# Scores of the first batch from turned q and k in float32, in one product instead of three float16 ones, and a larger weight of the longest chain in the order of work

## The chip, the cores and the metric

The kernel runs on one core of one Trainium2 chip. The metric is the device time of one execution in microseconds (us), the median of several runs. Lower is better.

## The reference

The program is attention with rotary position embedding, followed by a two-layer perceptron. There are 4 batches of 8 heads, 576 positions and 64 values per head:

```python
q_rot, k_rot = rotate(q), rotate(k)                # x1*cos - x2*sin, x1*sin + x2*cos
scores = q_rot @ k_rot.T / sqrt(64)
attn = exp(scores - max(scores)); attn /= sum(attn) + 1e-9
x = (attn @ v)                                     # all heads side by side: 2304 x 512
h = x @ w_in                                       # 2304 x 2048
out = (h * tanh(softplus(h))) @ w_out              # 2304 x 512
```

q and k have a standard deviation of about 0.58, and all inputs are float32.

## The kernel before, in words

**Layout.** Two heads make a pair P (16 pairs, four to a batch). The turned q and k of a pair lie with 128 partitions, 64 rows for each of its heads, and 576 columns. A step (P, t) makes 128 rows of scores for both heads (t = 0 to 3; 2 x 576 columns); the fifth, t = 4, holds the last 64 rows of both heads in one tile of 576 columns. Steps 0 and 1 make block 0 of a pair (256 tokens), steps 2 to 4 block 1 (320 tokens). All pairs of a batch do block 0 first, then block 1. The perceptron takes a batch in the same two blocks, so there are eight chunks of it; each needs the attention output of all four pairs of its block.

**Turning (`rope_turn`, line 387).** SP loads raw q or k (with the halves swapped beside it) into the tile raw0 or raw1, of which there is one each (L389). For batch 0 only, DVE takes its largest absolute value (L393). The products with cos and sin (L399) and their sum (L402), in two halves of 288 columns, run on POOL or DVE, whichever the planner finds sooner. The sum is written over the raw tile.

**Parts (`prep`, line 410).** A float32 number is written as two float16 parts, after a multiplication by a power of two. ScalarE (ACT) makes the first part (L418), DVE the second (L420), both from the raw tile into the tile qk. DVE then copies the last 64 columns of k of each head onto the diagonal of a tile kd (L427), so that one product with 128 rows makes the last 64 columns of the scores of both heads, the tails.

**The power of two (`max_exponents` line 359, `pow2` line 376, `qk_scale` line 684).** DVE reduces the largest values (L362), PE turns them into a row (L365), DVE reduces the row (L367), takes the exponent and bounds it (two L340), spreads it on a diagonal (L371), PE broadcasts it (L373), and DVE makes four factors (L340) and the factor `unit` that takes them back (L690). In batch 0 this runs once for each pair, in `prep_first` (line 675); later batches have one scale for a batch.

**Scores (`scores`, line 450).** Three float16 products (first by first, second by first, first by second part) go into PSUM for each head: 512 columns with 64 rows per head (L461), then the tails (L470). There are two PSUM tiles `psc`, which scores, the transposes of the weights and the first layer of the perceptron share. Then (`exponentials`, line 491) DVE takes the maximum (L495), ACT scales it (L497) and makes the exponentials (L501), both with `unit` as their scale, read from memory.

**Weights and values.** In batch 0 the weights stay float32: PE transposes them (L534, L536), ACT or DVE copies them out (L546, L547), and float32 products with v make the output (L610, L612, L613; L612 and L613 write the two column halves). Later batches use two float16 parts and DMA transposes (L583).

**Perceptron weights.** w_in and w_out come as 64-bit words in quarters and eighths (L779, L810) into tiles that are used for other things later. DVE takes their largest value (L697), PE and DVE find the power of two, and a decode of ACT, POOL and DVE instructions (L710, L718 or L719, L722, L725, then L731, L732, L735) makes two float16 parts. A buffer is free for the next load after L725 has read it. The layers themselves are L876 and L912, three float16 products each.

**The order.** All operations are recorded first, each with an estimated duration, the engines that may do it, and what it reads and writes. A planner (`Plan.order`, line 123) then simulates the engines and issues, on each, the ready operation of the lowest priority number. That number is the operation's place in the recorded order minus ALPHA times the length in us of the longest chain behind it. The issue order on each engine is fixed by it. ALPHA is 26. All loads go through SP's queue, in order.

Of the kernel before, what the change touches and what calls it, by code (L numbers as in the profile page):

```python
# [10 lines left out]
F32 = mybir.dt.float32  # L11
# [7 lines left out]
AF = mybir.ActivationFunctionType  # L19
# [15 lines left out]
RING = 4  # L35
# [9 lines left out]
QS = 0  # L45
NX = 4
TR = 107 / 128
ALPHA = 26
COUNT = [10, 10, 10, 10, 10, 10, 10, 0]
BURST = 2  # L50
SLOT0 = [15, 17, 18, 20, 22, 23, 25, 26, 28]
# [207 lines left out]
def dve_ns(n):  # L259
    return 1.04 * n + 65  # L260
# [23 lines left out]
def attention_mish_mlp(ctx: ExitStack, tc: tile.TileContext, qk, v, flat, rope, ident_in, w_in, w_out, outT):  # L284
# [11 lines left out]
    def fixed(shape, dt, name, planned=True):  # L296
        return Buf(lambda: const.tile(list(shape), dt, name=name), planned=planned)
# [12 lines left out]
    w2 = fixed((128, 4, 2, NF, 128), F16, "w2")  # L310
    w2e = [Buf(lambda e=e: w2()[:, e]) for e in range(4)]
    kdiag = [fixed((128, 2, 128), F16, f"kd{r}") for r in range(RING)]
    for t in (*kdiag, cs, ident, ones, cells, w1, w2):
        t()
    def psc():

# [5 lines left out]
    def small(shape=(128, 1), dt=F32):  # L322
        at = sc.get("n", 0)
        sc["n"] = at + shape[1]
        return Buf(lambda: cells()[0:shape[0], at:at + shape[1]].bitcast(dt))
# [61 lines left out]
    def rope_turn(P, j):  # L387
        t = sbuf((128, 2, S), F32, f"raw{j}", 1)
        load("qk", dma_ns(128 * 2 * S * 4), lambda dma: dma(t(), qk[P][:, 2 * j:2 * j + 2]),  # L389
             w=[(t, 0), (t, 1), (t, 2), (t, 3)])  # L390
        if P < NP:
            am = sc["qkam", P]
            op((DVE, dve_ns(S), lambda: nc.vector.tensor_reduce(  # L393
                am()[:, j:j + 1], t()[:, 0], axis=AX.X, op=ALU.max, apply_absolute_value=True)), w=[(am, j)], r=[(t, 0), (t, 1)])
        for c in range(2):
            s = slice(c * HS, (c + 1) * HS)

            def mul(e, s=s):
                e.tensor_tensor(out=t()[:, :, s], in0=t()[:, :, s], in1=cs()[:, :, s], op=ALU.mult)  # L399

            def add(e, s=s):
                e.tensor_tensor(out=t()[:, 0, s], in0=t()[:, 0, s], in1=t()[:, 1, s], op=ALU.add)  # L402

            op([(POOL, pool_ns(S), lambda f=mul: f(nc.gpsimd)), (DVE, dve_ns(S), lambda f=mul: f(nc.vector))],
               w=[(t, c), (t, 2 + c)], r=[cs], port=True)
            op([(POOL, pool_ns(HS), lambda f=add: f(nc.gpsimd)), (DVE, dve_ns(HS), lambda f=add: f(nc.vector))],
               w=[(t, c)], r=[(t, 2 + c)], port=True)
        return t

    def prep(P, j):  # L410


        t = st.pop(("T", P, j)) if P < NP else rope_turn(P, j)
        if j == 0:
            st["QK", P] = sbuf((128, 4, S), F16, "qk", RING)
        o = st["QK", P]
        s = sc["qk", P if P < NP else -(P // NP)][j]
        op((ACT, act_ns(S, ptr=1), lambda: nc.scalar.activation(o()[:, 2 * j], t()[:, 0], AF.Copy, scale=f32(s))),  # L418
           w=[(o, 2 * j)], r=[(t, 0), (t, 1), s])
        op((DVE, dve_ns(S) + 61, lambda: nc.vector.scalar_tensor_tensor(  # L420
            out=o()[:, 2 * j + 1], in0=t()[:, 0], scalar=f32(s), in1=o()[:, 2 * j], op0=ALU.mult, op1=ALU.subtract)),
           w=[(o, 2 * j + 1)], r=[(t, 0), (t, 1), s, (o, 2 * j)], port=True)
        if j == 1:
            d = st["KD", P] = Buf(kdiag[P % RING], [st["KD", P - RING]] if P >= RING else ())
            for h in range(2):
                own = slice(64 * h, 64 * h + 64)
                op((DVE, 200, lambda own=own: nc.vector.tensor_copy(d()[own, :, own], o()[own, 2:4, 512:S])),  # L427
                   w=[(d, h)], r=[(o, 2), (o, 3)], port=True)
# [21 lines left out]
    def scores(P, t):  # L450


        QK, kd = st["QK", P], st["KD", P]
        pt = psc()
        passes = ((0, 2), (1, 2), (0, 3))

        def fn():
            def mm(h, q, keys, to, rows=slice(0, 128)):
                own = slice(64 * h, 64 * h + 64)
                for a, (i, j) in enumerate(passes):  # L460
                    yield lambda a=a, i=i, j=j: nc.tensor.matmul(  # L461
                        pt()[rows, to:to + keys.stop - keys.start], QK()[own, i, q], QK()[own, j, keys], start=a == 0, stop=a == 2)

            if t < 4:
                q = slice(128 * t, 128 * t + 128)
                for one in zip(*[mm(h, q, slice(0, 512), 1024 * h) for h in range(2)]):
                    for f in one:
                        f()
                for a, (i, j) in enumerate(passes):
                    nc.tensor.matmul(tails(pt), QK()[:, i, q], kd()[:, j - 2], start=a == 0, stop=a == 2)  # L470
            else:
                q, A, B_ = slice(512, S), slice(0, 64), slice(64, 128)
                a = [*mm(0, q, slice(0, 512), 0, A), *mm(0, q, slice(512, S), 512, A)]
                b = [*mm(1, q, slice(0, 448), 64, B_), *mm(1, q, slice(512, S), 0, B_), *mm(1, q, slice(448, 512), 512, B_)]
                for f in (a[0], b[0], a[1], b[1], a[2], b[2], *b[3:6], a[3], b[6], a[4], b[7], a[5], b[8]):
                    f()

        op((PE, 6 * 150, fn), w=[pt], r=[(QK, k) for k in range(4)] + [(kd, h) for h in range(2)])
        return pt

    def both(pt, n):
# [4 lines left out]
    def tails(pt):  # L486

        x = pt()
        return bass.AP(tensor=x.tensor, offset=x.offset + 512, ap=[x.ap[0], [448, 2], [1, 64]])

    def exponentials(P, t, sm):
        n, unit = 2 if t < 4 else 1, sc["unit", P if P < NP else -(P // NP)]
        pt = scores(P, t)
        m = sbuf((128, 2), F32, "mx", 4)
        op((DVE, dve_ns(n * S), lambda: nc.vector.tensor_reduce(  # L495
            m()[:, :n], both(pt, n), axis=AX.X, op=ALU.max, negate=True)), w=[m], r=[pt])
        op((ACT, 220, lambda: nc.scalar.activation(m()[:, :n], m()[:, :n], AF.Copy, scale=unit())), w=[m], r=[unit])  # L497
        es = []
        for h in range(n):
            e = sbuf((128, S), F32, f"e{h}", 2)  # L500
            op((ACT, 850, lambda h=h, e=e: nc.scalar.activation(  # L501
                e(), pt()[:, 960 * h:960 * h + S], AF.Exp, bias=m()[:, h:h + 1],
                scale=unit(), accum_out=sm()[:, h:h + 1])), w=[e, (sm, h)], r=[pt, m, unit], table="exp")
            es.append(e)
        return es

# [167 lines left out]

    def prep_first(P):

        sc["qkam", P] = small((128, 2))
        for j in range(2):
            st["T", P, j] = rope_turn(P, j)
        qk_scale(P, 1)  # L680
        for j in range(2):
            prep(P, j)

    def qk_scale(b, n=3):

# [333 lines left out]

    nc.scalar.preload_act_table_set("exp_and_others")  # L1020
    nc.vector.memset(ones(), 1.0)
    for t in kdiag:
        nc.vector.memset(t(), 0.0)
    program()
    with tc.manual_schedule():
# [56 lines left out]
```

## Time and profile before

| | |
|---|---|
| median of 3 runs | 714.83 us (713.12 to 715.37) |
| the profiled execution | 716.38 us |
| its span, first to last instruction | 714.6 us |
| mean granted TensorE clock | 0.938 |
| busy: PE / DVE / ACT / POOL | 613.4 / 489.5 / 459.7 / 218.6 us |

PE is TensorE, DVE VectorE, ACT ScalarE, POOL GpSimd, SP the queue that issues the loads. A row of groups gives a line of the kernel, the engine, the operation, output and input tiles with their shapes, how often it ran, then the busy time in us and the mean of one in ns. A clock of 1.00 is 2.4 GHz, 0.50 is 1.2 GHz; values between are a mean over a stretch. Neighbouring instructions on an engine overlap a little in their recorded spans.

### The profile page before, as it was taken

To read this page: it belongs to the slowest core of one execution; us is meant where nothing else is said; L and a number is where in the kernel's file an instruction comes from. 1 tells how busy PE (TensorE), PEld (TensorE's weight loads), DVE (VectorE), ACT (ScalarE), POOL (GpSimd) and SP (SyncE) were. 2 spreads that over 40 slices of the span, in tenths; PEclk is the share of its full clock that TensorE was granted. 3 is DMA by queue.
4 is the path that set the end of the run, shared out by engine and by line. 5 is a ranking of instruction groups with operands and counts; after the bars stand their busy time and mean duration, and the time that the engine had idled before them with its cause. 6 is when DMAs were issued, how large, how long until landed. Compare 5 with 4: busy or idle time off the path is not lost.

```text
span 714.6 us, 13150 instructions
## 1 busy us (share of the span) xinstructions
PE 613.4 (86%) x5069; PEld 423.8 (59%) x5069; DVE 489.5 (69%) x904; ACT 459.7 (64%) x974; POOL 218.6 (31%) x209
## 2 busy tenths in 40 slices
PE   1446776975779999999979899999799999998997
PEld 0223444753456776677656566777566667776775
DVE  6999988798879586748956987478747584471210
ACT  2636778784667567758765776788657775682520
POOL 3344542115445411303551632024534020020000
PEclk9957886997789999999999999999999999999999
DMA  9824560350344584936598649456861294345000
GB/s 355 349 98 167 186 177 23 104 141 1 127 132 111 160 188 117 172 63 128 124 190 223 173 113 175 82 126 115 168 150 34 61 166 86 60 94 103 1 11 28
DMA packets 162416, 90.78 MB, mean 127 GB/s; under 512 B 129585, under 2 KB 150193, under 8 KB 162353
## 3 DMA queue, kind: packets, MB, share of 16 engines
q1 hardware_dynamic: 157744, 85.22, 49.3%
q10 hardware_dynamic: 4608, 4.72, 2.1%
q8 instruction: 40, 0.66, 0.4%
q14 instruction: 24, 0.19, 0.1%
HBM read 53.35 MB, written 4.72 MB: 81 GB/s over the span
## 4 chain that ended last, share of the span: by engine, by line
PE 53%; DVE 22%; DMA 11%; ACT 9%; issue 3%; SPq 1%; POOL 0%; POOLq 0%; ACTq 0%; DVEq 0%
PE psc L876 19%; PE pp L912 16%; PE psc L461 5%; PE po L622 4%; DVE mx L495 3%; DMA et<-ew 3%; ACT e L501 3%; DMA w<-in_w_out 3%; DMA stg<-in_v 2%; PE po L912 2%; DVE ew L522 2%; DVE mr L725 2%; DVE cells L697 2%; DVE qk L420 1%; PE psc L470 1%
## 5 line engine op out<-in xcount | busy, mean ns | idle before, releaser
L876 PE MATMUL psc<-xt,w 128*128 128x256 f16 (+1 forms) x1536 | 195.7, 287 | 6.8 <-ACT mh L880 4.3
L912 PE MATMUL pp<-g,w 128*128 128x256 f16 (+1 forms) x1440 | 190.4, 287 | 8.4 <-ACT ot L920 4.4
L876 PEld LDWEIGHTS <-w 128*128 128x128 f16 x1536 | 150.3, 98 | 47.6 <-issue 9.4
L912 PEld LDWEIGHTS <-w 128*128 128x128 f16 x1536 | 147.6, 98 | 50.6 <-issue 14.3
L501 ACT ACTIVATE e<-psc,mx,cells 128x576 f32<-128x576 f32 x144 | 118.3, 824 | 4.8 <-DVE ew L522 2.2
L516 POOL TENSOR_SCALAR ew<-e,rs 128x576 f16<-128x576 f32 x66 | 53.9, 823 | 220.0 <-DVE rs L512 201.5
L495 DVE TENSOR_REDUCE mx<-psc 128x2 f32<-128x1152 f32 (+1 forms) x80 | 98.0, 1231 | 24.5 <-PE psc L470 16.4
L522 DVE SCALAR_TENSOR_TENSOR ew<-e,rs,ew 128x576 f16<-128x576 f32 x108 | 92.5, 888 | 17.5 <-POOL ew L516 12.5
L880 ACT ACTIVATE mh<-psc,cells 128x256 f32<-128x256 f32 (+1 forms) x128 | 62.7, 498 | 62.2 <-PE psc L876 57.9
L897 DVE SCALAR_TENSOR_TENSOR g<-mh,cells,g 128x512 f16<-128x512 f32 (+1 forms) x64 | 58.1, 910 | 59.5 <-ACT g L894 59.2
L399 POOL TENSOR_TENSOR raw<-raw,cs 128x576 f32<-128x576 f32 x45 | 69.3, 1555 | 70.9 <-DMA raw<-in_qk 51.5
L461 PE MATMUL psc<-qk 64*128 64x512 f16 (+3 forms) x624 | 73.6, 356 | 14.0 <-ACT e L501 8.4
L497 ACT ACTIVATE mx<-mx,cells 128x2 f32<-128x2 f32 (+1 forms) x80 | 23.4, 292 | 49.1 <-DVE mx L495 48.2
L735 POOL TENSOR_TENSOR w<-mr,w 128x512 f16<-128x512 f32 x22 | 26.5, 1210 | 83.3 <-ACT w L731 67.2
L461 PEld LDWEIGHTS <-qk 64*128 64x128 f16 (+1 forms) x624 | 26.1, 102 | 42.7 <-issue 25.9
L623 PE MATMUL po<-et,v 128*64 128x320 f16 (+1 forms) x288 | 46.7, 301 | 0.5 <-DMA et<-ew 0.5
L402 POOL TENSOR_TENSOR raw<-raw 128x288 f32<-128x288 f32 x49 | 43.8, 912 | 11.0 <-DVE raw L399 8.2
L622 PE MATMUL po<-et,v 128*64 128x320 f16 (+1 forms) x288 | 47.0, 301 | 0.0
L894 ACT ACTIVATE g<-mh,cells 128x640 f16<-128x640 f32 (+1 forms) x59 | 45.8, 776 | 1.7
L518 ACT ACTIVATE ew<-e,rs 128x576 f16<-128x576 f32 x42 | 31.7, 767 | 11.7 <-DMA et<-ew 5.9
L666 DVE TENSOR_REDUCE cells<-stg 128x1 f32<-128x768 f32 x30 | 28.0, 944 | 15.6 <-DMA stg<-in_flat 15.6
L622 PEld LDWEIGHTS <-v 128*64 128x64 f16 x288 | 28.6, 113 | 14.1 <-issue 9.4
(102 smaller groups left out, 787.7 us busy)
## 6 DMA issues: line engine op xcount, KB each, us to landing
raw<-in_qk SPq DMA_DIRECT2D x32, 576.0 KB, 4.5
stg<-in_flat SPq DMA_DIRECT2D x30, 384.0 KB, 3.8
w<-in_w_in SPq DMA_DIRECT2D x6, 1024.0 KB, 12.7
w<-in_w_out SPq DMA_DIRECT2D x5, 1024.0 KB, 5.9
stg<-in_v SPq DMA_DIRECT2D x12, 320.0 KB, 3.7
stg<-in_w_out SPq DMA_DIRECT2D x6, 512.0 KB, 4.5
out_dram<-ot ACTq DMA_DIRECT2D x16, 160.0 KB, 2.8
g<-in_w_in SPq DMA_DIRECT2D x2, 1024.0 KB, 9.1
```

The costliest lines, as they stand in the source:

```text
L399: e.tensor_tensor(out=t()[:, :, s], in0=t()[:, :, s], in1=cs()[:, :, s], op=ALU.mult)
L461: yield lambda a=a, i=i, j=j: nc.tensor.matmul(pt()[rows, to:to + keys.stop - keys.start], QK()[own, i, q], QK()[own, j, keys], start=a == ...
L495: op((DVE, dve_ns(n * S), lambda: nc.vector.tensor_reduce(m()[:, :n], both(pt, n), axis=AX.X, op=ALU.max, negate=True)), w=[m], r=[pt])
L501: op((ACT, 850, lambda h=h, e=e: nc.scalar.activation(e(), pt()[:, 960 * h:960 * h + S], AF.Exp, bias=m()[:, h:h + 1], scale=unit(), accum ...
L516: op([(POOL, 1.27 * S, lambda: nc.gpsimd.tensor_scalar(w()[:, c], e(), r()[:, h:h + 1], 1.0, op0=ALU.mult, op1=ALU.mult)), (ACT, act_ns(S, ...
L522: op((DVE, dve_ns(S) + 61, lambda: nc.vector.scalar_tensor_tensor(out=w()[:, c], in0=e(), scalar=r()[:, h:h + 1], in1=w()[:, hc], op0=ALU. ...
L622: nc.tensor.matmul(po()[0:64, :n], V()[:, vi, c, 0:64], et[:, c, :n], start=False, stop=last)
L623: nc.tensor.matmul(po()[64:128, :n], V()[:, vi, c, 64:128], et[:, 5 + c, :n], start=False, stop=last)
L876: nc.tensor.matmul(hp(), w1()[:, wi, cc, f:f + 128], x()[:, xi, cc], start=cc == 0 and a == 0, stop=cc == NCC - 1 and a == 2)
L880: op((ACT, act_ns(n, psum=True, ptr=1), lambda j=j, hp=hp: nc.scalar.activation(hn()[:, j, :n], hp(), AF.Mish, scale=uh())), w=[(hn, j)], ...
L897: op((DVE, dve_ns(2 * n) + 61, lambda: nc.vector.scalar_tensor_tensor(out=out(1), in0=hn()[:, :, :n], scalar=f32(gs), in1=out(0), op0=ALU. ...
L912: nc.tensor.matmul(pp()[:, :n], w2e[e]()[:, wi, f], g()[:, gi, f % 8, :n], start=f == 0 and a == 0, stop=f == NF - 1 and a == 2)
```

## The change

Pairs 0 to 3 (P < NX = 4, the first batch) keep turned q and k in float32. The largest values, the powers of two and the float16 parts are gone for them; the sum of the rotation writes straight into the tile qk, which is now float32 of the same size. A float32 tile per pair holds the diagonal. One float32 product per head and one for the tails make the scores, and the constant 1/8 takes the place of `unit`. The planner's estimate for the scores of such a step goes from 900 to 1100 ns, and ALPHA from 26 to 35, for all operations of the kernel.

```diff
-ALPHA = 26
+ALPHA = 35
...
+    kwide = [fixed((128, 128), F32, f"kw{r}") for r in range(NX)]
...
 def rope_turn(P, j):
...
-        if P < NP:
-            am = sc["qkam", P]
-            op((DVE, dve_ns(S), lambda: nc.vector.tensor_reduce(
-                am()[:, j:j + 1], t()[:, 0], axis=AX.X, op=ALU.max, apply_absolute_value=True)), w=[(am, j)], r=[(t, 0), (t, 1)])
+        wide = st["QK", P] if P < NX else None
...
-                e.tensor_tensor(out=t()[:, 0, s], in0=t()[:, 0, s], in1=t()[:, 1, s], op=ALU.add)
+                e.tensor_tensor(out=wide()[:, j, s] if wide else t()[:, 0, s], in0=t()[:, 0, s], in1=t()[:, 1, s], op=ALU.add)
...
 def scores(P, t):
...
-        passes = ((0, 2), (1, 2), (0, 3))
+        exact = P < NX
+        passes = ((0, 1),) if exact else ((0, 2), (1, 2), (0, 3))
...
-                    nc.tensor.matmul(tails(pt), QK()[:, i, q], kd()[:, j - 2], start=a == 0, stop=a == 2)
+                    nc.tensor.matmul(tails(pt), QK()[:, i, q], kd() if exact else kd()[:, j - 2],
+                                     start=a == 0, stop=a == len(passes) - 1)
...
-                for f in (a[0], b[0], a[1], b[1], a[2], b[2], *b[3:6], a[3], b[6], a[4], b[7], a[5], b[8]):
+                for f in (a[0], *b[:2], a[1], b[2]) if exact else (a[0], b[0], a[1], b[1], a[2], b[2], *b[3:6], a[3], b[6], a[4], b[7], a[5], b[8]):
...
-        op((PE, 6 * 150, fn), w=[pt], r=[(QK, k) for k in range(4)] + [(kd, h) for h in range(2)])
+        op((PE, 1100 if exact else 6 * 150, fn), w=[pt], r=[(QK, k) for k in range(4)] + [(kd, h) for h in range(2)])
...
 def exponentials(P, t, sm):
-        n, unit = 2 if t < 4 else 1, sc["unit", P if P < NP else -(P // NP)]
+        n, unit = 2 if t < 4 else 1, None if P < NX else sc["unit", -(P // NP)]
+        units = [] if unit is None else [unit]
+
+        def scale():
+            return D ** -0.5 if unit is None else unit()
...
 def prep_first(P):
-        sc["qkam", P] = small((128, 2))
+        o = st["QK", P] = sbuf((128, 2, S), F32, "qk", RING)
         for j in range(2):
-            st["T", P, j] = rope_turn(P, j)
-        qk_scale(P, 1)
-        for j in range(2):
-            prep(P, j)
+            rope_turn(P, j)
+        d = st["KD", P] = kwide[P]
+        for h in range(2):
+            own = slice(64 * h, 64 * h + 64)
+            op((DVE, 150, lambda own=own: nc.vector.tensor_copy(d()[own, own], o()[own, 1, 512:S])),
+               w=[(d, h)], r=[(o, 3)], port=True)
...
-    for t in kdiag:
+    for t in (*kwide, *kdiag):
         nc.vector.memset(t(), 0.0)
```

## Rows read from the trace of the kernel before

**Rows 1.** Busy time of each engine by stage: the stage in us and its length; then for each engine the busy us and, in brackets, its instructions; then the mean granted clock of TensorE, the share of the DMA engines and GB/s.

```profile
0.00:9.00 9.00, 0.37 (x1) 0.08 (x1) 3.84 (x12) 1.28 (x1) 1.54 (x5) 1.00 0.81 305
9.00:98.00 89.00, 48.64 (x289) 28.11 (x291) 82.54 (x183) 51.72 (x113) 42.09 (x38) 0.78 0.60 219
98.00:222.00 124.00, 94.35 (x711) 62.53 (x708) 105.19 (x244) 88.02 (x205) 45.74 (x42) 0.82 0.33 95
222.00:660.00 438.00, 419.21 (x3700) 296.68 (x3698) 290.89 (x459) 300.60 (x629) 129.26 (x126) 0.99 0.61 128
660.00:714.60 54.60, 50.84 (x375) 36.40 (x372) 7.08 (x8) 18.05 (x29) 0.00 (x0) 1.00 0.04 15
```

The engines stand in the order PE, PE's weight loads, DVE, ACT, POOL.

**Rows 2.** The loads on SP's queue: two lines of the waits of the whole span (what waited, for what: us in total, times, longest us), then the issue of the third pair's raw q and k in order of time (start us, length us).

```profile
SPq L810 <- DVE mr L725: 83.5, 9, 28.1
SPq L389 <- DVE qk L420: 41.1, 8, 9.6
...
43.83 1.06 SPq L389 DMA_DIRECT2D raw<-in_qk  x2
```

**Rows 3.** DVE in order of time, with the first score product on PE: start us, length us, the instruction, and in brackets the idle time before it and what ended it. Neighbours of one kind are merged (x2, x4).

```profile
4.60 0.76 DVE L393 TENSOR_REDUCE cells<-raw 128x1 f32<-128x576 f32 x1 [3.05 <-DMA raw<-in_qk]
...
12.39 1.42 DVE L402 TENSOR_TENSOR raw<-raw 128x288 f32<-128x288 f32 x2
...
14.98 0.80 DVE L420 SCALAR_TENSOR_TENSOR qk<-raw,cells,qk 128x576 f16<-128x576 f32 x1
...
15.33 1.12 PE L461 MATMUL psc<-qk 64*128 64x512 f16 x4 [3.79 <-ACT qk L418]
...
16.96 0.80 DVE L420 SCALAR_TENSOR_TENSOR qk<-raw,cells,qk 128x576 f16<-128x576 f32 x1
...
18.55 0.57 DVE L427 COPY kd<-qk 64x128 f16<-64x128 f16 x2
...
20.35 1.35 DVE L495 TENSOR_REDUCE mx<-psc 128x2 f32<-128x1152 f32 x1
...
41.93 0.35 DVE L340 TENSOR_SCALAR cells<-po 128x1 int32<-128x1 f32 x4
...
42.98 1.55 DVE L420 SCALAR_TENSOR_TENSOR qk<-raw,cells,qk 128x576 f16<-128x576 f32 x2
```

**Rows 4.** Groups of DVE instructions in the first 80 us: busy us and mean ns, then the idle time before them. Of the 18 on `po`, 16 belong to the chains of the first batch.

```profile
L420 DVE SCALAR_TENSOR_TENSOR qk<-raw,cells,qk 128x576 f16<-128x576 f32 x8 | 6.3, 813 | 0.7 <-ACT qk L418 0.6
L393 DVE TENSOR_REDUCE cells<-raw 128x1 f32<-128x576 f32 x8 | 5.9, 745 | 3.7 <-DMA raw<-in_qk 3.7
L427 DVE COPY kd<-qk 64x128 f16<-64x128 f16 x8 | 2.0, 246 | 0.1
L371 DVE TENSOR_SCALAR cells<-ident,cells 2x2 f32<-2x2 f32 x4 | 1.8, 456 | 0.0
L340 DVE TENSOR_SCALAR cells<-po 128x1 int32<-128x1 f32 x18 | 1.7, 144 | 0.9 <-PE po L373 0.7 <-PE po L356 0.3
L367 DVE TENSOR_REDUCE cells<-po 2x1 f32<-2x128 f32 x4 | 1.1, 273 | 0.0
L690 DVE TENSOR_SCALAR cells<-cells 128x1 f32<-128x1 f32 x4 | 0.8, 207 | 0.0
L362 DVE TENSOR_REDUCE cells<-cells 128x2 f32<-128x2 f32 x4 | 0.6, 149 | 0.0
L340 DVE TENSOR_SCALAR cells<-cells 2x1 int32<-2x1 int32 x4 | 0.5, 134 | 0.0
```

**Rows 5.** PE in order of time: two steps' scores at full clock (88.33) and at half clock (83.38), float32 products on a column half (75.96 to 77.04, six of a run), and float32 transposes of 128 columns.

```profile
75.96 0.38 PE L612 MATMUL po<-et,v 128*64 128x256 f32 x1
75.97 0.38 PE L613 MATMUL po<-et,v 128*64 128x256 f32 x1
...
77.04 0.38 PE L612 MATMUL po<-et,v 128*64 128x256 f32 x1
...
78.79 1.04 PE L534 MATMUL psc<-ident,e 128*128 128x128 f32 x8
...
83.38 1.46 PE L461 MATMUL psc<-qk 64*128 64x512 f16 x6 [2.09 <-ACT e L501]
84.77 0.50 PE L470 MATMUL psc<-kd,qk 128*128 128x128 f16 x3
...
88.33 0.82 PE L461 MATMUL psc<-qk 64*128 64x512 f16 x6
89.09 0.34 PE L470 MATMUL psc<-kd,qk 128*128 128x128 f16 x3
```

**Rows 6.** Groups of ACT instructions in the first 150 us (of the ten L418, eight are the first batch's): busy us and mean ns, then the idle time before them. L710, L497 and L418 read their scale from memory, L719 and L510 have constants.

```profile
L710 ACT ACTIVATE mr<-w,cells 128x512 f32<-128x512 f32 x12 | 8.9, 755 | 2.8 <-POOL w L735 2.7
L719 ACT ACTIVATE w<-w 128x512 int32<-128x512 uint32 x13 | 8.3, 674 | 5.3 <-DMA w<-in_w_in 3.3 <-DMA w<-in_w_out 2.0
L418 ACT ACTIVATE qk<-raw,cells 128x576 f16<-128x576 f32 x10 | 7.3, 768 | 2.3 <-DVE raw L402 1.4 <-DVE cells L340 0.9
L497 ACT ACTIVATE mx<-mx,cells 128x2 f32<-128x2 f32 x12 | 3.6, 296 | 8.7 <-DVE mx L495 8.7
L510 ACT ACTIVATE sm<-sm 128x2 f32<-128x2 f32 x12 | 2.4, 203 | 0.2
```

**Rows 7.** The two stretches of 40 us behind 222 us in which PE idles most; columns as in rows 1.

```profile
340.00:380.00 40.00, 34.98 (x325) 24.66 (x322) 28.88 (x56) 26.78 (x62) 20.19 (x19) 0.96 0.78 165
500.00:540.00 40.00, 34.48 (x284) 23.36 (x281) 24.71 (x32) 24.60 (x47) 21.64 (x19) 0.96 0.67 142
```

More of the change, by code (lines that the diff above doesn't have):

```diff
@@ L312, in attention_mish_mlp @@
     kdiag = [fixed((128, 2, 128), F16, f"kd{r}") for r in range(RING)]
-    for t in (*kdiag, cs, ident, ones, cells, w1, w2):
+    kwide = [fixed((128, 128), F32, f"kw{r}") for r in range(NX)]
+    for t in (*kdiag, *kwide, cs, ident, ones, cells, w1, w2):
         t()
@@ L406, in rope_turn @@
             op([(POOL, pool_ns(HS), lambda f=add: f(nc.gpsimd)), (DVE, dve_ns(HS), lambda f=add: f(nc.vector))],
-               w=[(t, c)], r=[(t, 2 + c)], port=True)
+               w=[(wide, 2 * j + c) if wide else (t, c)], r=[(t, 2 + c)] + [(t, c)] * bool(wide), port=True)
         return t
     def prep(P, j):
-        t = st.pop(("T", P, j)) if P < NP else rope_turn(P, j)
+        t = rope_turn(P, j)
         if j == 0:
@@ L416, in prep @@
         o = st["QK", P]
-        s = sc["qk", P if P < NP else -(P // NP)][j]
+        s = sc["qk", -(P // NP)][j]
         op((ACT, act_ns(S, ptr=1), lambda: nc.scalar.activation(o()[:, 2 * j], t()[:, 0], AF.Copy, scale=f32(s))),
@@ L461, in mm @@
                     yield lambda a=a, i=i, j=j: nc.tensor.matmul(
-                        pt()[rows, to:to + keys.stop - keys.start], QK()[own, i, q], QK()[own, j, keys], start=a == 0, stop=a == 2)
+                        pt()[rows, to:to + keys.stop - keys.start], QK()[own, i, q], QK()[own, j, keys], start=a == 0, stop=a == len(passes) - 1)
             if t < 4:
@@ L496, in exponentials @@
             m()[:, :n], both(pt, n), axis=AX.X, op=ALU.max, negate=True)), w=[m], r=[pt])
-        op((ACT, 220, lambda: nc.scalar.activation(m()[:, :n], m()[:, :n], AF.Copy, scale=unit())), w=[m], r=[unit])
+        op((ACT, 220, lambda: nc.scalar.activation(m()[:, :n], m()[:, :n], AF.Copy, scale=scale())), w=[m], r=units)
         es = []
@@ L502, in exponentials @@
                 e(), pt()[:, 960 * h:960 * h + S], AF.Exp, bias=m()[:, h:h + 1],
-                scale=unit(), accum_out=sm()[:, h:h + 1])), w=[e, (sm, h)], r=[pt, m, unit], table="exp")
+                scale=scale(), accum_out=sm()[:, h:h + 1])), w=[e, (sm, h)], r=[pt, m, *units], table="exp")
             es.append(e)
```

## The prediction

> **What bounds the kernel now.** First the busy time by stage [rows 1]: the span falls in two halves. From 9 to 98 us VectorE (DVE) is busy 82.5 of 89 us, TensorE (PE) only 48.6, at a mean granted clock of 0.78; from 98 to 222 us DVE has 105.2 of 124 us and PE 94.4; from 222 us PE has 419.2 of 438 us at 0.99 and is the bound to the end. So what shortens the front moves the end almost one for one, if PE gets no new work or holes behind it. Next the queue that feeds the front [rows 2]: loads of w_out wait 83.5 us for DVE's last decode step L725, loads of raw q and k wait 41.1 us (later batches included) for DVE's L420. Buffers come free when DVE gets round to them. Last, DVE in order of time [rows 3]: the rows of a first-batch pair (largest value L393, second part L420, diagonal L427, maximum L495) stand in a queue without gaps. The first scores start at 15.33 us and the first maximum at 20.35 us, because L420 and L427 come between them.
>
> **What is removed on DVE.** For each of the four pairs of batch 0 [rows 4]: two L393 of 745 ns, two L420 of 813 ns, and the chain of powers of two: L362 149, two L340 on two partitions of 134 each (the second kind is like the row), L367 273, L371 (456 in the mean), four L340 on the product 144 each, L690 207 ns. In durations that is 4 x (1.49 + 1.63 + 1.93) = 20 us. They overlap: two L420 stand in 1.55 us and four L340 in 0.35 us [rows 3], so the next one starts about 0.07 us before the end. Start to start I count 0.67, 0.74 and, per chain, some 1.0 us (+1.0 once, for the first L371): 8 x 0.67 + 8 x 0.74 + 4.9 = 16.2 us. The first two reductions and their L362, 1.4 us, lie before 9 us, where DVE waits for the data anyway (3.05 us idle ahead of the first [rows 3]); removed in the window: **14.8 us**.
>
> **What that is worth.** 82.5 - 14.8 = 67.7 us of DVE work remain. At the density of now (82.5/89) they take 73 us, a gain of 16.0; at the density of the next stage (105.2/124 = 0.85), where chains and loads bind as much as DVE, 79.8 us, a gain of 9.2 [rows 1]. I take 12, near the middle, since PE (48.6) and ScalarE (51.7, less eight L418 of 768 ns = 45.6 [rows 6]) stay well under 75 us, so DVE remains first but no longer without gaps. The stage from 98 us on is the same work, started earlier: its w_out loads are released by L725, which moves with DVE.
>
> **What is added.** Four more zero fills on DVE at the start lie in the same 3.05 us of waiting: nothing. If that cover went, 0.2 us each, by the size of an L427 [rows 4]. The copies of the diagonal remain, eight of 64x64 float32 for eight of 64x128 float16; not shown, between half of and the same as the 246 ns of now [rows 4]: nothing. The sum of the rotation now writes another tile: same engine and size, nothing. No wait is new in it: pairs 0 to 3 are the first users of the four slots. The raw tile is free after that sum and not after L420, so the raw loads of pair 1 to 3, on SP's queue, go out earlier, by some 4 us if the first pair is typical (its sums end at 13.8 us, its L420 at 17.8; the third pair's loads were issued at 43.83, between the L420 of 42.98 to 44.53 [rows 2, 3]); what was queued behind them on SP (parts of v for the maxima, weights) goes earlier too. That is part of the density above and isn't counted again.
>
> **Scores on PE.** A step's six float16 products of 512 columns take 0.76 us at full clock (88.33 to 89.09) and 1.39 at half (83.38 to 84.77), the two heads side by side [rows 5]. One float32 product of 256 columns leaves two records; pairs of them, on two column halves at once, start every 0.216 us (five in 75.96 to 77.04). So 512 columns cost two records of 0.43 = 0.86 us, if row halves run side by side as column halves do. The tails: two records like the transposes of L534, eight in 1.04 us, 0.25 us, against three in some 0.17. So a step costs **+0.2 us at full clock, up to +0.55 at half**; the fifth tile of a pair has the same columns per head, so all 20 steps alike: 4 to 11 us of PE, half of it before 98 us under DVE. The Trainium skill, "Perfetto Trace Analysis", section Engine Utilization, halves TensorE's rate for its low-high float32 mode; by that alone 512 columns would take 0.43 us, a step would get 0.3 us cheaper, and the sum below would be 4 us lower. The rows fit a half rate for each record, but there are two records for each product, so I don't take it.
>
> **ScalarE on the same path.** Maximum and exponentials lose their scale read from memory and get a constant. Bound by nearest rows [rows 6]: 512 elements with a pointer 755, with a constant 674 ns; 128x2 with a pointer 296, with constants 203. So 0.09 us each, three to a step, -0.27 us. Between nothing and that; with PE's +0.2 to +0.55 a step's chain changes by -0.07 to +0.55. Over the ten or so steps behind 98 us that is -1 to +5.5; PE idles 30 of the 124 us there [rows 1], so I take **+1**.
>
> **The order.** The weight of the longest chain goes from 26 to 35 for every operation; no row shows what that does. The nearest: behind 222 us PE idles 438 - 419.2 = 19 us, and the two worst stretches of 40 us lose 5.0 and 5.5 us [rows 1, 7]. So a gain of at most 19, a loss of one hole like these, 5.5, for each that opens. I take 0, as PE there is nearly full under either order.
>
> **Sum.** -12 + 1 + 0 = -11 us. The profiled execution took 716.38 us (span 714.6 and 1.8 around it): 705.4. It lies 1.55 us above the median of the three runs, 714.83, so the forecast for a median is **703.8 us** (-1.5%). With both ends of DVE (9.2 to 16.0) and of the step chain (+5.5 to -1) it runs from -17 to -4, 698 to 711.
>
> **Rivals.** *A, the gain is lost behind 98 us.* There w_out comes in quarters, each load waiting for the decode of one before [rows 2]; if that chain or the two score buffers set the pace whatever DVE has free, only the earlier start of the first pair is kept: first maximum 20.35 us now, against sums that end at 13.8 us [rows 3] plus a diagonal and a step's scores at half clock, 2.5 us, so 4 us, minus PE's +1 to +4: -3 to 0, **711.8 to 715**. For it: DVE's density falls to 0.85 there; against it: the loads wait for DVE, not for the memory. *B, slower: float32 products on the two row halves don't run side by side.* No row shows them. Then each step costs 0.86 us more at full clock and 1.7 at half, with the rest 1.1 to 2.2; at the 0.82 of 98 to 222 us about 1.5, on ten steps 15 us in a stage where PE has little room; those before 98 us stay under DVE. -11 + 15 = +4: **719**, up to 726 if half of the first ten show too. It decides from 1.1 us a step on. Against it: float16 rows of L461 and float32 column halves both overlap [rows 5]. The Trainium skill, "TensorEngine Tiling", Key Properties, says that tiles operate independently; no run here shows that for float32 on row halves. *C, the new order opens holes behind 222 us:* two of 5.5 us give -11 + 11, **715**; three 720. *D, more than forecast:* the order closes some holes, and PE, idle less, keeps the full clock in the front: -17 to -25, **690 to 698**. For it: the granted clock of 0.78 and 0.82 [rows 1].
>
> **How the numbers follow.** Forecast 0.55; A 0.15 (two thirds of it faster, one third within the bound); B 0.08; C 0.12 (half within, half slower); D 0.10. A measurement of this kernel tells no less than 0.3% (2.1 us) from no change. Faster: 0.55 + 0.10 + 0.10 + a little = 0.76; within: 0.05 + 0.06 = 0.11; slower: 0.08 + 0.05 = 0.13. The range leaves out the end of D and most of B and the worse half of C: **693 to 717**.
>
> **What would show it.** Right: no L393, L420 or chain rows for pairs 0 to 3; the first maximum at about 15 to 16 us; PE's nearly full stage starting at some 211 us, not 222; score products of 512 columns in records with two heads at once, 0.9 to 1.0 us a step at full clock; ScalarE's 128x2 scaling at about 200 ns. Wrong: score products one after another (1.7 us at full clock: B); DVE with gaps from 9 to 98 us while w_out is loaded at the old times (A); the full stage earlier but PE's idle time behind it above 25 us (C).

## The result and the profile after

The changed kernel takes 701.45 us (median of 4 runs, 697.82 to 702.21) against 713.98 us for the kernel before beside it; the ratio is **0.984, 95% interval 0.980 to 0.987**. The medians differ by 12.5 us; 11 were forecast. The profiled execution took 701.27 us, its span is 699.5 us, its mean clock 0.948. In what follows, a difference between two kernels is that of their ratios to the kernel before, times 712 us; worked out from the two intervals, it is uncertain by some 3 to 4 us either way. For the change itself that difference is 11.5 us.

Busy time by stage, columns as in [rows 1] (stage, length, then PE, PE's weight loads, DVE, ACT, POOL with instruction counts, clock, DMA share, GB/s), for the changed kernel:

```profile
0.00:9.00 9.00, 0.00 (x0) 0.00 (x0) 3.32 (x13) 1.28 (x1) 0.32 (x5) 1.00 0.79 292
9.00:98.00 89.00, 57.56 (x287) 31.68 (x289) 81.99 (x156) 44.77 (x109) 42.50 (x40) 0.79 0.65 230
98.00:222.00 124.00, 97.52 (x717) 65.74 (x714) 104.76 (x246) 80.53 (x190) 48.27 (x42) 0.86 0.33 88
222.00:660.00 438.00, 422.05 (x3728) 298.63 (x3726) 289.99 (x462) 308.87 (x638) 121.49 (x114) 1.00 0.60 128
660.00:699.50 39.50, 36.01 (x266) 25.72 (x263) 3.54 (x4) 9.14 (x15) 0.00 (x0) 0.99 0.05 17
```

Against [rows 1], PE's busy time over the whole span is the same (613.4 before, 613.1 us after), so the gain is idle time of PE. It is the same although the scores got longer, since other products took less: those for the powers of two are gone, and the 128 transposes of the weights up to 222 us took 318 ns each instead of 340, at a mean granted clock of 0.83 instead of 0.81 from 9 to 222 us. Up to 222 us PE idles 66.9 us where it idled 78.6, behind that 19.4 us instead of 22.6. DVE from 9 to 98 us is as full as it was, 82.0 of 89 us: other work filled what was removed. Which work, groups of DVE in that stage show, first before, then after (products of the rotation L399 and L397, its sums L402 and L400):

```profile
L399 DVE TENSOR_TENSOR raw<-raw,cs 128x576 f32<-128x576 f32 x5 | 4.8, 983 | 0.0
L402 DVE TENSOR_TENSOR raw<-raw 128x288 f32<-128x288 f32 x9 | 5.5, 653 | 0.0
```

```profile
L397 DVE TENSOR_TENSOR raw<-raw,cs 128x576 f32<-128x576 f32 x11 | 8.7, 840 | 1.0 <-DMA raw<-in_qk 1.0
L400 DVE TENSOR_TENSOR qk<-raw 128x288 f32<-128x288 f32 x8 | 6.4, 843 | 0.0
```

The rotation has 4.8 us more of DVE, with 11 products instead of 5; POOL made 7 of them up to 98 us, where it had made 14. The largest values and the decode of the weights together have 5.1 us more (28.3 instead of 23.2; L704, L729 and L732 against L697, L722 and L725), copies out of PSUM 2.7 (6.9 instead of 4.2), and one more maximum 1.4. The last decodes of the perceptron's weights stand further on (durations least/median/largest, then first and last start), before (L725) and after (L732):

```profile
L725 DVE SCALAR_TENSOR_TENSOR mr<-stg,mr x2: 665/672/679, 226.5 to 227.1; 128x512 int32<-128x512 int32 x2
```

```profile
L732 DVE SCALAR_TENSOR_TENSOR mr<-stg,mr x6: 667/684/807, 171.1 to 213.3; 128x512 int32<-128x512 int32 x6
```

The last of 32 decodes starts at 213.3 instead of 227.1 us, 13.8 us earlier. The steps of attention came earlier too, but did not keep the lead. The third, the eighth and the twelfth step's scores on PE, before (the eighth, at 83.38, stands in [rows 5]) and after:

```profile
45.95 1.46 PE L461 MATMUL psc<-qk 64*128 64x512 f16 x6
...
106.76 0.82 PE L461 MATMUL psc<-qk 64*128 64x512 f16 x6 [1.46 <-ACT e L501]
```

```profile
33.65 2.08 PE L460 MATMUL psc<-qk 64*128 64x512 f32 x4 [1.89 <-DVE qk L400]
...
77.00 2.08 PE L460 MATMUL psc<-qk 64*128 64x512 f32 x4 [4.04 <-DVE mr L732]
...
106.16 2.08 PE L460 MATMUL psc<-qk 64*128 64x512 f32 x4 [3.96 <-ACT e L506]
```

That is 12.3, 6.4 and 0.6 us earlier; the perceptron's first product starts at 119.2 instead of 121.8 us. So the freed time went first to the steps and in the end mostly to the weights. Why the steps lost their lead (longer scores, or weights placed ahead of them) is not shown.

DVE at the start, in order of time, answers to [rows 3]:

```profile
9.56 2.50 DVE L400 TENSOR_TENSOR qk<-raw 128x288 f32<-128x288 f32 x2
11.99 0.38 DVE L688 COPY kw<-qk 64x64 f32<-64x64 f32 x2
...
15.05 1.35 DVE L500 TENSOR_REDUCE mx<-psc 128x2 f32<-128x1152 f32 x1
```

There is no largest value, no chain and no second part; the first maximum starts at 15.05 us, 5.3 earlier. The scores on PE, two steps at full clock (84.37) and half (91.36), answer to [rows 5], and two groups of ACT in the first 150 us to [rows 6]:

```profile
84.37 1.13 PE L460 MATMUL psc<-qk 64*128 64x512 f32 x4
85.43 0.49 PE L469 MATMUL psc<-kw,qk 128*128 128x128 f32 x2
...
91.36 2.01 PE L460 MATMUL psc<-qk 64*128 64x512 f32 x4 [1.70 <-ACT e L506]
93.30 0.79 PE L469 MATMUL psc<-kw,qk 128*128 128x128 f32 x2
```

```profile
L506 ACT ACTIVATE e<-psc,mx 128x576 f32<-128x576 f32 x25 | 18.3, 737 | 0.2
L502 ACT ACTIVATE mx<-mx 128x2 f32<-128x2 f32 x12 | 2.4, 204 | 19.6 <-DVE mx L500 19.6
```

The waits of the loads on SP's queue, and the issue of the third pair's raw q and k, answer to [rows 2] (what waited, for what: us, times, longest us); L817 loads w_out, L390 raw q and k, L418 makes the second parts, which only later batches still have:

```profile
SPq L817 <- DVE mr L732: 86.6, 9, 27.5
SPq L390 <- DVE qk L418: 23.6, 8, 5.7
...
34.87 0.80 SPq L390 DMA_DIRECT2D raw<-in_qk  x2
```

The loads of w_out still wait for the decode. The raw loads' wait for the parts fell from 41.1 to 23.6 us, all their waits together from 62 to 54; the third pair's were issued 9 us earlier, the fourth's 15 (45.95 instead of 60.74). On PE, four records (two heads, two each) take 1.06 us at full clock, from their start to that of the tails; one after another they would take 4 x 0.43 = 1.7 by [rows 5]. So the heads do run side by side.

### The profile page after: what moved, and what is told of

It is laid out like the page before. It is cut to its first block, busy times and chain, and to the rows that moved or that the text cites. A ratio compares the mean times of both kernels' runs of the same rounds, so it can differ in the third digit from the quotient of the medians.

```text
span 699.5 us, 12922 instructions
## 1 busy us (share of the span) xinstructions
PE 613.1 (88%) x4989; PEld 421.8 (60%) x4989; DVE 483.6 (69%) x879; ACT 444.6 (64%) x949; POOL 212.6 (30%) x199
## 4 chain that ended last, share of the span: by engine, by line
PE 61%; DVE 18%; DMA 8%; ACT 8%; issue 2%; SPq 2%; POOL 0%; POOLq 0%; ACTq 0%; DVEq 0%
PE psc L883 21%; PE pp L919 18%; PE psc L460 8%; PE po L627 3%; DMA et<-ew 3%; DVE mx L500 3%; PE psc L469 2%; PE po L617 2%; PE po L919 2%; DMA w<-in_w_out 2%; DVE mr L729 2%; DMA g<-in_w_in 2%; ACT e L506 2%; DVE ew L527 1%; DVE mr L732 1%
## 5 line engine op out<-in xcount | busy, mean ns | idle before, releaser
L883 PE MATMUL psc<-xt,w 128*128 128x256 f16 (+1 forms) x1536 | 195.2, 286 | 12.9 <-ACT mh L887 10.9
L460 PE MATMUL psc<-qk 64*128 64x512 f16 (+4 forms) x572 | 82.6, 405 | 28.8 <-DVE qk L400 14.1
L904 DVE SCALAR_TENSOR_TENSOR g<-mh,cells,g 128x512 f16<-128x512 f32 (+1 forms) x64 | 53.4, 836 | 57.0 <-ACT g L901 56.6
L506 ACT ACTIVATE e<-psc,mx,cells 128x576 f32<-128x576 f32 x108 | 89.1, 828 | 4.8 <-DVE ew L527 3.5
L397 POOL TENSOR_TENSOR raw<-raw,cs 128x576 f32<-128x576 f32 x37 | 57.6, 1564 | 61.5 <-DMA raw<-in_qk 61.4
L742 POOL TENSOR_TENSOR w<-mr,w 128x512 f16<-128x512 f32 x26 | 31.8, 1233 | 62.0 <-ACT w L738 41.6
L901 ACT ACTIVATE g<-mh,cells 128x512 f16<-128x512 f32 (+1 forms) x58 | 45.1, 777 | 1.8
L628 PE MATMUL po<-et,v 128*64 128x320 f16 (+1 forms) x288 | 44.2, 290 | 0.7 <-DMA et<-ew 0.7
L627 PE MATMUL po<-et,v 128*64 128x320 f16 (+1 forms) x288 | 44.7, 290 | 0.0
L397 DVE TENSOR_TENSOR raw<-raw,cs 128x576 f32<-128x576 f32 x27 | 23.6, 897 | 18.5 <-DMA raw<-in_qk 18.4
L502 ACT ACTIVATE mx<-mx,cells 128x2 f32<-128x2 f32 (+1 forms) x60 | 17.6, 293 | 28.6 <-DVE mx L500 28.2
L400 POOL TENSOR_TENSOR raw<-raw 128x288 f32<-128x288 f32 x34 | 32.7, 976 | 4.3 <-ACT g L901 3.1
```

Of the source, the lines that this page charges most:

```text
L460: yield lambda a=a, i=i, j=j: nc.tensor.matmul(pt()[rows, to:to + keys.stop - keys.start], QK()[own, i, q], QK()[own, j, keys], start=a == ...
L506: op((ACT, 850, lambda h=h, e=e: nc.scalar.activation(e(), pt()[:, 960 * h:960 * h + S], AF.Exp, bias=m()[:, h:h + 1], scale=scale(), accu ...
L627: nc.tensor.matmul(po()[0:64, :n], V()[:, vi, c, 0:64], et[:, c, :n], start=False, stop=last)
L883: nc.tensor.matmul(hp(), w1()[:, wi, cc, f:f + 128], x()[:, xi, cc], start=cc == 0 and a == 0, stop=cc == NCC - 1 and a == 2)
L901: op([(ACT, act_ns(2 * n, ptr=1), lambda: nc.scalar.activation(out(0), hn()[:, :, :n], AF.Copy, scale=f32(gs))), (DVE, dve2_ns(2 * n, ptr= ...
L904: op((DVE, dve_ns(2 * n) + 61, lambda: nc.vector.scalar_tensor_tensor(out=out(1), in0=hn()[:, :, :n], scalar=f32(gs), in1=out(0), op0=ALU. ...
```

## The experiments

Each run is compared with the kernel before on the same chip. A run is called different where the intervals of the ratios don't overlap.

**One part alone: the order.** The weight is one number, so each half of the change can be run without the other.

```diff
-ALPHA = 35
+ALPHA = 26
```

> The changed kernel with the old weight of the longest chain (26), so with another order of all work. Theory (the freed VectorE time in the front carries the gain, the order is worth nothing by itself): 700 to 706 us, as the changed kernel's 701.5. Rival (the new order carries most of it): 710 to 716 us, near the kernel before.

Measured: 703.88 us, ratio 0.989 (0.986 to 0.993).

The other half, on the kernel before:

```diff
-ALPHA = 26
+ALPHA = 35
```

> The kernel before with the new weight (35) alone: float16 parts and powers of two stay. Theory: 711 to 718 us, within 0.5% of the kernel before on either side. Rival (the order carries it): 702 to 706 us.

Measured: 718.23 us, ratio 1.008 (1.005 to 1.011): 6 us slower. So the float32 scores alone, at the old weight, make 7.7 us, and the new weight alone loses 5.7. "Nothing by itself" is wrong for the kernel before. On the changed kernel the weight adds 3.8 us by the ratios, but the intervals touch (0.980 to 0.987 and 0.986 to 0.993). The halves don't add up: at the new weight, the float32 scores make 17.2 us (1.008 to 0.984), at the old one 7.7. Two more weights:

```diff
-ALPHA = 35
+ALPHA = 30        # and, in the other run, 40
```

> The changed kernel with weight 30. Theory (an order is one draw from a scatter of some 4 us to either side, without a trend in the weight): between 697 and 706 us, not on a line between 703.9 (26) and 701 (35). Rival (a larger weight suits the shorter chains of the changed kernel): 701.5 to 704 us, between the two.

> The changed kernel with weight 40. Theory (scatter, as for 30): 697 to 706 us. Rival (a larger weight suits it): 698 to 701 us, below weight 35.

Measured: 701.33 us, ratio 0.985 (0.983 to 0.988), and 702.61 us, ratio 0.986 (0.983 to 0.989). On the changed kernel 30, 35 and 40 are alike; 26 is slower than they are by 2 to 4 us, with intervals that overlap. Both times lie in the range of the theory (scatter) and outside that of the rival (a trend with the weight), but by less than the uncertainty, so neither is shown. The stages to 222 us and to 660 us, columns as above, first of weight 35, then of weight 26, both with float32 scores, then of weight 35 with parts:

```profile
0.00:222.00 222.00, 155.08 (x1000) 97.41 (x1001) 190.08 (x413) 126.59 (x297) 91.09 (x85) 0.84 0.47 154
```

```profile
0.00:222.00 222.00, 160.85 (x1054) 104.22 (x1055) 200.00 (x414) 139.23 (x322) 96.16 (x86) 0.89 0.51 166
222.00:660.00 438.00, 416.63 (x3664) 293.65 (x3663) 286.81 (x456) 299.82 (x627) 108.57 (x105) 0.99 0.58 122
```

```profile
0.00:222.00 222.00, 141.31 (x985) 90.67 (x986) 189.06 (x440) 131.61 (x291) 96.29 (x88) 0.81 0.45 150
222.00:660.00 438.00, 418.19 (x3694) 294.32 (x3693) 301.53 (x469) 307.03 (x642) 131.21 (x120) 0.99 0.60 129
```

With float32 scores, weight 26 gets 5.8 us more PE work done in the front, and loses 5.4 us to idle time between 222 and 660 us. With parts, weight 35 did 2 us less in the front than weight 26 in [rows 1], and had 1 us more idle time from 222 to 660 us. These are single executions.

**VectorE's time in the front, given back.** Same issue order on every engine; only the instructions of an existing operation grow.

```diff
+        dose = small((128, 4))
...
+            def diag(own=own, h=h):
+                for j in range(2):
+                    nc.vector.tensor_reduce(dose()[:, 2 * h + j:2 * h + j + 1], o()[:, j], axis=AX.X, op=ALU.max, apply_absolute_value=True)
+                nc.vector.tensor_copy(d()[own, own], o()[own, 1, 512:S])
+
-            op((DVE, 150, lambda own=own: nc.vector.tensor_copy(d()[own, own], o()[own, 1, 512:S])),
-               w=[(d, h)], r=[(o, 3)], port=True)
+            op((DVE, 150, diag), w=[(d, h)], r=[(o, 3)], port=True)
```

> The changed kernel, the same issue order on every engine, with four more VectorE reductions of 576 columns ahead of each of the first four pairs' diagonal copies (16 in all, about 0.67 us each start to start, 10.7 us; their results are not used). They stand where the largest values and second parts stood. Theory: the front is VectorE's, so 8 to 11 us come back: 709 to 713 us. Rival A (loads of w_out or the score buffers set the pace of the front whatever VectorE has free): 701 to 704 us.

Measured: 710.49 us, ratio 0.998 (0.995 to 1.000), so 9.7 us come back. The added row:

```profile
L691 DVE TENSOR_REDUCE cells<-qk x16: 729/736/743, 11.3 to 65.4; 128x1 f32<-128x576 f32 x16
```

16 x 0.67 = 10.7 us of DVE between 11 and 66 us cost 9.7 us: 0.9 us for each, and 0.6 to 1.2 with the uncertainty. This is the theory's number; rival A (the pace set by loads or buffers) falls. One thing this run can't split: the dose stands where the removed work stood, ahead of the diagonal that a pair's scores wait for. So it fills DVE and also lengthens a pair's chain; PE's wait for the diagonal rose from 1.6 to 6.0 us between 9 and 98 us, and the eighth step's scores started at 86.60 instead of 77.00 us.

**The same dose later.**

```diff
 def prep(P, j):
...
+                    if 8 <= P < 12:
+                        for j in range(2):
+                            nc.vector.tensor_reduce(sc["dose"]()[:, 2 * h + j:2 * h + j + 1], cs()[:, j], axis=AX.X, op=ALU.max, apply_absolute_value=True)
                     nc.vector.tensor_copy(d()[own, :, own], o()[own, 2:4, 512:S])
```

> The changed kernel, the same issue order, with the 16 added VectorE reductions of the dose run moved to the third batch's diagonal copies (pairs 8 to 11, about 280 to 400 us), reading the cos and sin tile; results not used. Theory (VectorE's time counts only in the front; behind 222 us TensorE is the bound): 700 to 703.5 us. Rival (VectorE's time counts wherever it is spent, since the steps' chains run through it): 707 to 712 us.

Measured: 707.44 us, ratio 0.992 (0.989 to 0.995): 5.9 us slower than the changed kernel. The theory that DVE's time is free behind 222 us falls. The stretch in which the 16 stood (319.9 to 395.3 us), of the changed kernel and then of this run:

```profile
300.00:420.00 120.00, 112.28 (x985) 78.40 (x982) 89.12 (x148) 89.44 (x182) 43.04 (x40) 1.00 0.67 151
```

```profile
300.00:420.00 120.00, 106.66 (x923) 74.86 (x921) 96.30 (x156) 83.59 (x168) 40.74 (x37) 0.99 0.63 145
```

PE loses 5.6 us here, nearly the whole loss. The mean of DVE looked free (89 of 120 us). In slices of 20 us, two hold most of it; first the changed kernel, then this run:

```profile
320.00:340.00 20.00, 20.00 (x195) 14.23 (x194) 17.57 (x30) 16.08 (x36) 8.21 (x7) 1.00 0.56 140
380.00:400.00 20.00, 18.06 (x145) 11.74 (x144) 18.54 (x26) 14.41 (x27) 10.57 (x10) 1.00 0.59 185
```

```profile
320.00:340.00 20.00, 18.15 (x176) 12.74 (x174) 19.70 (x28) 14.58 (x34) 7.72 (x7) 1.00 0.47 111
380.00:400.00 20.00, 14.79 (x118) 9.33 (x116) 19.88 (x26) 11.92 (x23) 8.38 (x8) 0.97 0.51 164
```

There DVE had 17.6 and 18.5 of 20 us, the dose takes it to 19.7 and 19.9, and PE loses 1.9 and 3.3 us. A full DVE is not PE's only limit here: from 360 to 380 us of the changed kernel PE idles 2.9 us while DVE has 9.5 of 20.

**The constant scale on ScalarE.**

```diff
+    eighth = fixed((128, 1), F32, "eighth", planned=False)
...
-            return D ** -0.5 if unit is None else unit()
+            return eighth() if unit is None else unit()
...
+    nc.vector.memset(eighth(), D ** -0.5)
```

> The changed kernel, the same issue order, with the constant 1/8 read from a cell in memory by the maximum's scaling and the exponentials of the first batch, as before. Theory: those instructions get 0.09 us longer each (56 of them, 5 us of ScalarE), of which a fifth to a half is on the path of the steps: 702 to 704.5 us. Rival (ScalarE has room everywhere): within 1 us of the changed kernel, 700.5 to 702.5.

Measured: 700.75 us, ratio 0.983 (0.980 to 0.986): no difference. The exponentials took 824 ns and the scalings 293 again, so the size of the term was right, 0.09 us each. Its worth can't be told from nothing; the theory's +1 to +3 us is not ruled out by an uncertainty of 3 us, though the measured -0.7 lies nearer to the rival.

**Float32's time on TensorE, doubled and taken away.**

```diff
+        def twice():
+            fn()
+            if exact:
+                fn()
+
-        op((PE, 1100 if exact else 6 * 150, fn), w=[pt], ...
+        op((PE, 1100 if exact else 6 * 150, twice), w=[pt], ...
```

> The changed kernel, the same issue order, with all score products of the first batch issued twice (the second overwrites the first). By the records of the changed kernel a step's scores take 1.4 us of TensorE at full clock (1.06 and 0.3 for the tails) and 2.6 at half, so 20 steps add 28 to 52 us of TensorE, nearly all of it ahead of 222 us, where TensorE idles 67 us. Theory (VectorE is the front's bound, TensorE's room takes part of it, but the later steps and the score buffers wait): a quarter to a half shows, 710 to 722 us. Rival 1 (all under VectorE): 701 to 704 us. Rival 2 (TensorE's time counts in full, as float32's extra cost then would): 728 us or more.

Measured: 717.45 us, ratio 1.008 (1.005 to 1.011): 17.3 us more than the changed kernel, for 29.3 us of PE busy time (642.5 against 613.1 in all): 0.6 us for each. The stage from 9 to 98 us of this run, and in that stage the wait of DVE's maximum for the scores, of the changed kernel and then of this run:

```profile
9.00:98.00 89.00, 64.03 (x303) 32.76 (x303) 71.16 (x141) 39.26 (x94) 37.64 (x36) 0.85 0.62 222
```

```profile
DVE mx L500 <- PE psc L469: 1.2, 3, 0.7
...
DVE mx L505 <- PE psc L469: 13.1, 7, 3.4
```

DVE falls to 71.2 of 89 us: with this much score time, DVE waits for PE, 13.1 us.

```diff
...
+        def single(a):
+            return a.bitcast(mybir.dt.bfloat16).rearrange("p (s t) -> p s t", t=2)[:, :, 1] if exact else a
...
-                        pt()[...], QK()[own, i, q], QK()[own, j, keys], ...
+                        pt()[...], single(QK()[own, i, q]), single(QK()[own, j, keys]), ...
...
-                    nc.tensor.matmul(tails(pt), QK()[:, i, q], kd() if exact else ...
+                    nc.tensor.matmul(tails(pt), single(QK()[:, i, q]), single(kd()) if exact else ...
```

> The changed kernel, the same issue order, with the first batch's score products made of the top 16 bits of each float32 number alone (as bfloat16; the low halves are left out of the scores): one record of a quarter of the length in place of two. By the double-product run a set of float32 scores is 29 us of TensorE's busy time and costs 16 us, 0.55 per us; this takes some 20 us away. Theory (float32's length on TensorE is on the front's path): 10 us less, 689 to 696 us. Rival (the front is VectorE's, and shorter scores find it busy; the double product only hurt because it made TensorE the bound): 698 to 702 us.

Measured: 697.28 us, ratio 0.979 (0.976 to 0.982). That is 3.5 us less than the changed kernel, with intervals that overlap: between the two ranges, and far from the 10 us of the theory. PE's busy time in all fell by 20.7 us (592.4 against 613.1), so some 0.17 us for each, with an uncertainty as large. TensorE's time in the front is cheap where it is shortened and dear where it is lengthened; float32's extra over three float16 products lies between the two. Neither busy time is score time alone, since PE's clock moved with it. From 9 to 98 us the mean granted clock was 0.79 in the changed kernel, 0.85 with the scores doubled and 0.71 with the top halves, and the same 128 transposes of the weights took (changed kernel, doubled, top halves, up to 222 us):

```profile
L539 PE MATMUL psc<-ident,e 128*128 128x128 f32 x128 | 21.0, 318 | 3.3 <-ACT ew L551 1.9 <-DVE rs L517 0.9 <-ACT e L506 0.5
L544 PE MATMUL psc<-ident,e 128*128 128x128 f32 x128 | 18.6, 293 | 0.3 <-ACT e L511 0.3
L542 PE MATMUL psc<-ident,e 128*128 128x128 f32 x128 | 22.3, 332 | 8.3 <-ACT ew L554 5.6 <-ACT e L509 2.7
```

**Another way to relieve VectorE.** The planner had given 36 of the copies out of PSUM in the first 222 us to DVE (14.5 us in durations). Here all go to ACT, in the same recorded and issued sequence.

```diff
-            self.ops[n]["ways"][k][2]()
+            self.ops[n]["ways"][0 if self.ops[n].get("first") else k][2]()
...
                 (DVE, dve_ns(m), lambda: nc.vector.tensor_copy(out(), src()))], w=[(buf, part)], r=[pt])
+            plan.ops[-1]["first"] = True
```

> The changed kernel, the same recorded and issued order, with all copies of turned weights and sums out of PSUM on ScalarE, of which VectorE had 36 in the first 222 us (14.5 us in durations, some 12 start to start). Theory (0.9 us of time per us of VectorE in the front, ScalarE's time free as the constant scale showed): 8 to 11 us less, 690 to 694 us. Rival (the copies of a step now stand one behind the other on ScalarE and hold the score buffer and the exponentials behind them): 699 to 706 us.

Measured: **692.59 us, ratio 0.971 (0.967 to 0.976)**, 8.9 us below the changed kernel and the fastest of all runs; its intervals don't touch the changed kernel's. The front of this run (the profiled execution took 696.9 us):

```profile
9.00:98.00 89.00, 61.76 (x318) 35.12 (x318) 79.61 (x150) 50.71 (x132) 45.06 (x41) 0.81 0.69 242
98.00:222.00 124.00, 103.16 (x753) 70.49 (x754) 104.57 (x223) 91.13 (x218) 54.15 (x46) 0.86 0.34 98
```

PE was busy for 164.9 us by 222 us where the changed kernel had 155.1, DVE is nearly as full as before, and the perceptron's first product starts at 112.5 instead of 119.2 us. This relief of DVE takes nothing out of a pair's chain ahead of its scores, which speaks for a price of DVE's time apart from that chain. The same edit on the kernel before:

> The kernel before, in its own recorded and issued order, with the copies out of PSUM on ScalarE as in the run on the changed kernel. Theory (VectorE is the bound of the front in both kernels, 0.9 us of time per us; ScalarE, with eight more conversions here, still has room): 6 to 11 us less than the kernel before, 702 to 707 us. Rival (in the kernel before the powers of two, not VectorE's total, held the steps): within 3 us of it, 709 to 715 us.

Measured: 708.2 us, ratio 0.995 (0.993 to 0.997), 3.7 us less, for 25 copies (10.9 us in durations): between the two expectations. DVE was still full there (81.9 of 89 us), and ACT fuller than in the run on the changed kernel (55.5 and 93.6 us in the two stages, against 50.7 and 91.1). That a relief of DVE paid with ACT's time is worth less where ACT also makes the parts would explain it, but is not shown. The rival's cause is there as well: in this run PE still idles 15.1 us up to 222 us ahead of the two products of the powers of two (L365 and L373). And one step further on the changed kernel:

```diff
...
+            if 0 < P < NX:
+                plan.ops[-1]["first"] = plan.ops[-2]["first"] = True
```

> The changed kernel with the copies on ScalarE and, besides, all products and sums of the rotation of pairs 1 to 3 on GpSimd (VectorE had about ten of each in the first batch, some 12 us). Theory (VectorE's time is the price): 5 to 9 us below the copies run's 692.6, 684 to 688 us. Rival (GpSimd takes twice as long for them, a pair's rotation gets 5 us longer and comes late for its steps): 692 to 700 us.

Measured: 699.55 us, ratio 0.982 (0.980 to 0.985): 7.5 us slower than the copies alone. DVE came down to 70.1 of 89 us, and the time went up. POOL and the third step's scores on PE in this run, and those scores in the run with the copies alone:

```profile
27.74 4.14 POOL L397 TENSOR_TENSOR raw<-raw,cs 128x576 f32<-128x576 f32 x3
31.83 3.04 POOL L400 TENSOR_TENSOR qk<-raw 128x288 f32<-128x288 f32 x4
34.92 2.08 PE L462 MATMUL psc<-qk 64*128 64x512 f32 x4 [5.38 <-POOL qk L400]
```

```profile
32.86 1.13 PE L460 MATMUL psc<-qk 64*128 64x512 f32 x4 [2.29 <-POOL qk L400]
```

The scores of pair 1 wait 5.4 us for POOL, which takes 7.1 us (27.74 to 34.87) for three of that pair's products and its sums. They start 2.1 us later than with the copies alone, the sixth step's 7.1 (67.63 against 60.57) and the perceptron's first product 7.9 (120.4 against 112.5): the whole loss is there by then. The rival holds: DVE's time is not the price when what takes its place lengthens the chain of the steps.

## Why the prediction held, point by point

- **The DVE removed (14.8 us), right, and its worth, somewhat small.** I took 12 us, in the middle between the density of now and that of the next stage. The dose gives 0.9 us per us, so 14.8 x 0.9 = 13.3 us; with the dose's uncertainty, 9 to 17, which holds the 12. The reason for the discount failed: DVE did not get gaps from 9 to 98 us (82.0 against 82.5 us busy [rows 1]), since the order had rotation, weights and copies to put there. The raw loads came 9 and 15 us earlier for the third and fourth pair, where the forecast had some 4.
- **Scores on PE, too small by a third to over a half.** I forecast +0.2 us a step at full clock to +0.55 at half. The rows give 1.06 us to the start of the tails and 0.49 for them, against 0.76 and 0.34 [rows 5]: +0.45; at half clock 1.94 and 0.79 against 1.39 and 0.50, +0.84. The estimate from column halves (0.86) left out 0.2 us at full clock, and the tails 0.07. Side by side was right. The Trainium skill's page "Perfetto Trace Analysis", Engine Utilization, halves the rate for low-high float32; by an estimate from that rate a step would have become cheaper by 0.3. The trace does not agree with it for a whole product. For a single record it does: 256 columns start every 0.216 us [rows 5], or half a column per tick at 2.4 GHz.
- **ScalarE, the size right, the worth not seen.** 823 to 737 and 296 to 204 ns are the forecast 0.09 us. Given back, they cost no time that the runs can tell, so nothing shows that they set off PE's extra, as the sum had it. PE's extra is probably worth more than the +1 I took: by 20 steps of 0.45 to 0.84 us (9 to 17 us) at 0.17 to 0.6 us each, +2 to +10. That is a range worked out from two runs, not a measurement.
- **The order, forecast as 0, is not nothing.** It is +5.7 us on the kernel before, and on the changed kernel 0 to -4, not settled. The float32 part alone measured -7.7 us. It fits 13.3 of DVE less some 5.6 of PE, inside that range; the 5.6 is what is left over and was not measured by itself. So the sum of -11 came out at -11.5 with a DVE term short by 1, a PE term short by some 5, and an order term that brought most of the latter back. At weight 35 the float32 part measures -17.2 us, so such a split into terms holds for one order only. The likeliest case held and DVE's term carried it; that the total agrees so much better than its terms is luck.
- **The rivals.** A: the loads of w_out wait for DVE's decode and start 12 us earlier (79.2 instead of 91.3), and the dose shows that DVE's work sets the pace; what did happen of A is that attention's steps had lost their lead by the first perceptron product (2.6 us earlier). B: the four records in 1.06 us rule out heads one after another. A step got dearer by 0.45 and 0.84 us, not by B's 1.1 to 2.2. C: two new holes did not open; idle time behind 222 us fell from 22.6 to 19.4 us. D: the clock in the front rose little (0.79 and 0.86, from 0.78 and 0.82), and the time did not reach it.
- **The signs named ahead.** First maximum at 15.05 us (15 to 16 forecast); PE is full from about 215 us (211 forecast): 5.00 of 5 us in each slice from 215 to 245 us. The 222 given for before is the end of a stage; read in the same slices, the kernel before is full from 230 us, so the move is 15 us. ScalarE's scaling took 204 ns (200 forecast), and a step's products of 512 columns 1.06 us (0.9 to 1.0 forecast).

What stays open: what the weight of 35 is worth on the changed kernel alone, and why it loses on the kernel before. An order can't be changed in one place with this planner, and single executions show front and holes moving by 1 to 6 us, against each other on the changed kernel, together on the kernel before. How much of DVE's price is its total time and how much a pair's chain is not split either; the copies speak for the first, the rotation on GpSimd for the second.

## What to carry to other kernels

Price an engine by a dose: the same order, a few added instructions of known length in an operation that is already there; here that gave 0.9 us per us of VectorE in the front. A dose also prices the chain that it stands in, so give one in a second place, or take the same engine's work away elsewhere. Read an engine's load in slices as short as the stages really are: a mean of 89 in 120 us hid two slices of 17.6 and 18.5 in 20, where most of the same dose's cost of 0.55 us per us arose. Removing work from a full engine does not make it idle; find out which work the order moves up, and whether that work has anybody waiting for it.

## What the runs showed that was not expected

- TensorE's time in the front had two prices: 0.6 us per us where score time was doubled, about 0.17 where it was cut. DVE was busy 71 of 89 us in the first run and 84.6 in the second, and PE's mean granted clock there was 0.85 and 0.71; which of the two makes the difference is not shown.
- The float32 scores were worth 7.7 us under one order of the work and 17.2 under another.
- Moving work from VectorE to ScalarE (36 copies) paid 8.9 us in the changed kernel; moving the rotation of three pairs from VectorE to GpSimd cost 7.5 us, although it emptied VectorE more (70.1 against 79.6 of 89 us).
